# Pooling V on GpSimd instead of TensorE from group 7 on, with slack in a list schedule

## The chip, the core and the metric

One core of a Trainium2 chip runs the whole program. Times are device microseconds of one execution. Each figure is a median of several runs. A ratio is the mean time of one kernel's fast runs over the mean of the other kernel's fast runs of the same rounds, so it is not quite the ratio of the medians quoted beside it. The kernel before spreads by 0.9 to 2.2% in the four sets of its runs (352.6 to 360.3 us in the widest), so the ratios carry a 95% interval of about half a per cent to one per cent each way. In that widest set, which serves e1 to e4, three of seven runs (358.1 to 360.3 us) lie over 1.5% above the fastest, are classed slow and are left out, though their granted clock (0.98 to 0.99) is like that of the others; with them the ratios of e1 to e4 would be about 0.006 lower. Engines: PE is TensorE, ACT is ScalarE, DVE is VectorE, POOL is GpSimd, SP issues the DMAs (SPq in a trace is its queue).

## The reference, cut to what matters

```python
# 8 batches, 8 heads, 576 tokens, head size 64; factor 4
v_d = v.reshape(B, H, Sd, factor, D).mean(axis=3)     # the pooled V of this change; q_d, k_d likewise
out_d = sm_attn(q_d, k_d, v_d)                        # 144 pooled tokens
out_up = np.repeat(out_d, factor, axis=2)
scores = np.where(np.abs(pos[:, None] - pos[None, :]) < factor, scale * q @ k.T, -1e9)
x = out_up + softmax(scores) @ v                      # -> (4608 tokens, 512)
h = x @ w_in                                          # 512 x 2048
out = (h - np.tanh(h)) @ w_out                        # 2048 x 512
```

## The kernel before

The attention works on 32 pairs of heads, two pairs to a group, so 16 groups of four heads. The dense part works on nine blocks of 512 tokens and needs the attention's `xT` of the batches in its block. All work is entered into a small list scheduler. Each operation has an engine, an assumed duration, a priority and its dependencies. The scheduler plans start times and emits each engine's instructions in that order. On the chip each engine then works through its own stream in order and waits where it must (e1 below shows it).

```python
LAT = {"PE": 270, "ACT": 150, "DVE": 110, "POOL": 150, "SP": 50, "DMA": 1800}
...
            for u in users[i]:                       # in order(): when may a user start?
                same = self.ops[u][0] == eng and eng != "DMA"
                at[u] = max(at[u], end if same else end + self.LAT[eng])
...
    def pool_v(hb):                                  # V of a group pooled on PE
        def mm():
            for t in range(NT):                      # NT = 5
                T.matmul(pv[:, 0, :], pick[:, t, :], vw[w][:, :, t, 0:64], ...)
            T.matmul(pv[:, 1, :], pick[:, 5, :], vw[w][:, :, 4, 0:64], start=True, stop=True)
        op("PE", 750, mm, ..., writes=["ox"], pri=20 * hb - 1)       # takes PSUM bank ox
        op("ACT", 300, lambda: A.copy(out=vd[w][:, :, :, 0:64], in_=pv...), ...)
...
    def load_v4(n): ...          # V once more, as rows of four tokens, into qkn buffer 2
    def sum_v(n): ...            # two pairwise adds on POOL, the second writes vd
...
        if p % 2 == 0 and 1 < n < GV:
            pool_v(n)
...
        if nl[0] >= GV:
            load_v4(nl[0])
            sum_v(nl[0])
```

With `GV = 99` the last branch is never taken. After the output matmuls of a pair, DVE takes reciprocals and normalises into `ln`, which frees bank `ox`; SP issues a DMA transpose of `ln` into `lnT` (pairs 12 and up), and DVE adds the pooled part of `lnT`, each value repeated four times, to the rest of it, and writes `xT`. With `MERGE = 14`, the scores of pairs 14 and up go into both banks, `ts` and `ox`, in one block, so they wait for that same normalisation.

The softmax here doesn't subtract the row's maximum and nothing guards it: scores larger than these inputs give would overflow.

## Time and profile before

| | before |
|---|---|
| median of the three timed runs | 356.5 us (353.5 to 356.6) |
| span of the profiled run | 351.9 us |
| PE busy, and its idle time | 331.2 us, 20.7 us |
| PE idle from 140 to 260 us | 5.2 us |
| DVE / ACT / POOL busy | 212.5 / 210.8 / 110.9 us |

The prediction below reads this profile and shows the lines. One caution on reading them: this profile holds 1107 of the 1152 dense matmuls (556 + 551 rows), so a few of PE's short gaps are missing records and not idle time.

### The profile page before, as it was taken

What the parts mean: (1) busy time and instruction counts of PE and PEld (TensorE: products, weight loads), DVE (VectorE), ACT (ScalarE), POOL (GpSimd) and SP (SyncE); (2) the same over time, 40 slices, a digit from 0 to 9 for tenths busy, and PEclk for the clock granted to TensorE, in tenths of its full rate; (3) what the DMA queues carried; (4) which work ended last, traced back from release to release, by engine and by line L of the source; (5) the groups of instructions that cost most, each with busy time, mean ns of one, the idle gap of its engine ahead of it and who ended that gap; (6) DMA issues with size and microseconds to landing.
All of it is one profiled execution on the core that took longest, in us unless ns stands there. A gap on an engine that the chain in (4) does not pass through costs nothing.

```text
span 351.9 us, 6824 instructions
## 1 busy us (share of the span) xinstructions
PE 331.2 (94%) x2624; PEld 175.0 (50%) x2670; DVE 212.5 (60%) x360; ACT 210.8 (60%) x353; POOL 110.9 (32%) x140
## 2 busy tenths in 40 slices
PE   6978999989999999899989999999999999999995
PEld 2553555545555555455545555555444444444442
DVE  4774875748959676666767776956764343334300
ACT  2765988567966767565756767667634343444421
POOL 8434846664442152543434262622000000000000
PEclk9996999999999999999999999999999999999999
DMA  6999999999201759293939576525220100010012
GB/s 210 259 387 268 294 371 294 255 245 310 72 32 29 204 134 259 69 254 48 250 74 251 145 190 174 149 58 81 59 59 30 59 31 31 30 60 32 30 68 83
DMA packets 79278, 52.21 MB, mean 148 GB/s; under 512 B 62350, under 2 KB 62350, under 8 KB 79246
## 3 DMA queue, kind: packets, MB, share of 16 engines
q1 hardware_dynamic: 79246, 51.78, 54.3%
q8 instruction: 21, 0.34, 0.4%
q14 instruction: 11, 0.09, 0.1%
HBM read 37.74 MB, written 9.44 MB: 134 GB/s over the span
## 4 chain that ended last, share of the span: by engine, by line
PE 61%; DMA 15%; DVE 9%; SPq 8%; ACT 3%; issue 2%; POOL 1%; POOLq 0%; ACTq 0%; DVEq 0%
PE ps_hy L686 26%; PE ps_hy L658 26%; DMA lnT<-ln 4%; SPq L340 3%; SPq L364 3%; DMA vst<-in_v_dram 3%; DMA gT<-in_moe_w_out_dram 3%; DMA gT<-in_moe_w_in_dram 3%; DVE ln L592 2%; DVE gT L670 2%; PE ps_ts L452 2%; PE ps_ts L503 2%; PE ps_ox L575 2%; DMA qkn<-in_k_dram 2%; PE ps_ox L414 1%
## 5 line engine op out<-in xcount | busy, mean ns | idle before, releaser
L658 PE MATMUL ps_hy<-xT,w_in_sb 128*128 128x512 bf16 x556 | 143.8, 383 | 5.5 <-DVE xT L635 3.0
L686 PE MATMUL ps_hy<-w_out_sb,gT 128*128 128x512 bf16 x551 | 140.8, 379 | 1.6 <-issue 0.5
L670 DVE TENSOR_TENSOR gT<-ps_hy,uy 128x512 bf16<-128x512 f32 x144 | 96.7, 686 | 74.7 <-ACT uy L667 73.9
L667 ACT ACTIVATE uy<-ps_hy 128x512 f32<-128x512 f32 x144 | 84.1, 600 | 81.6 <-PE ps_hy L658 76.8
L658 PEld LDWEIGHTS <-w_in_sb 128*128 128x128 bf16 x576 | 54.0, 98 | 64.3 <-issue 6.7
L686 PEld LDWEIGHTS <-gT 128*128 128x128 bf16 x576 | 53.3, 98 | 58.4
L468 POOL TENSOR_TENSOR half<-qk 128x576 f32<-128x576 bf16 x29 | 35.2, 1215 | 78.4 <-ACT qk L458 72.1
L458 ACT COPY qk<-ps_ts 128x1152 bf16<-128x1152 bf16 x28 | 31.5, 1126 | 10.1 <-PE ps_ts L452 8.2
L542 ACT ACTIVATE E<-ps_ts 128x960 bf16<-128x960 f32 x30 | 29.0, 970 | 7.3 <-PE ps_ts L503 7.0
L592 DVE TENSOR_TENSOR ln<-ps_ox,r 128x896 bf16<-128x896 f32 x30 | 32.7, 1090 | 0.9
L697 ACT COPY uy<-ps_hy 128x512 f32<-128x512 f32 x36 | 21.1, 585 | 19.5 <-PE ps_hy L686 18.3
L399 POOL CAST vw<-vst 128x640 bf16<-128x640 f32 x31 | 23.5, 761 | 13.4 <-DMA vst<-in_v_dram 9.9
L546 DVE TENSOR_TENSOR E<-E,mask 128x960 bf16<-128x960 bf16 x28 | 21.3, 762 | 8.0 <-ACT E L542 7.7
L452 PEld LDWEIGHTS <-qr 128*128 128x128 bf16 x288 | 19.6, 103 | 11.0 <-DVE qr L436 5.6
L436 POOL CAST qr<-qkn 128x1152 bf16<-128x1152 f32 x14 | 16.0, 1144 | 24.9 <-DMA qkn<-in_k_dram 18.3
L611 DVE TENSOR_TENSOR xT<-lnT 128x480 bf16<-128x480 bf16 (+1 forms) x40 | 19.5, 495 | 6.7 <-DMA lnT<-ln 6.7
L436 DVE CAST qr<-qkn 128x1152 bf16<-128x1152 f32 x18 | 14.4, 801 | 13.6 <-DMA qkn<-in_q_dram 8.6
L473 POOL TENSOR_TENSOR qkd<-half 128x288 bf16<-128x288 f32 x30 | 21.7, 725 | 2.6 <-DVE half L468 1.3
L452 PE MATMUL ps_ts<-ident,qr 128*128 128x128 bf16 x252 | 19.6, 225 | 2.2 <-POOL vd L760 1.3
L575 PE MATMUL ps_ox<-vw,E 128*128 128x65 bf16 x300 | 18.8, 194 | 2.0 <-DVE E L564 1.9
L575 PEld LDWEIGHTS <-E 128*128 128x128 bf16 x300 | 15.6, 98 | 9.1 <-DVE E L564 2.5
L503 PEld LDWEIGHTS <-qk 64*128 64x128 bf16 x320 | 9.6, 96 | 15.7 <-issue 12.4
(83 smaller groups left out, 239.1 us busy)
## 6 DMA issues: line engine op xcount, KB each, us to landing
vst<-in_v_dram SPq DMA_DIRECT2D x62, 160.0 KB, 5.0
qkn<-in_q_dram SPq DMA_DIRECT2D x32, 288.0 KB, 3.4
qkn<-in_k_dram SPq DMA_DIRECT2D x32, 288.0 KB, 4.9
out_dram<-uy SPq DMA_DIRECT2D x36, 256.0 KB, 2.3
gT<-in_moe_w_in_dram SPq DMA_DIRECT2D x4, 1024.0 KB, 9.3
xT<-in_moe_w_out_dram SPq DMA_DIRECT2D x8, 256.0 KB, 4.4
gT<-in_moe_w_out_dram SPq DMA_DIRECT2D x2, 1024.0 KB, 9.6
lnT<-ln SPq DMA_TRANSPOSE x20, 3.0
```

Source lines behind the costliest of these rows:

```text
L399: P.choice([(eng, ns, lambda fn=fn: fn(out=vw[w][:, 2 * jj:2 * jj + 2, :, 0:64], in_=vst[s])) for eng, ns, fn in CAST_V[p >= NEARLY]], rea ...
L436: P.choice([(eng, ns, lambda fn=fn: fn(out=dst, in_=srt)) for eng, ns, fn in REORDER[n >= 2][i]], reads=[("qkn", sn, i, x) for x in range(2)],
L452: T.transpose(b16[:, 128 * a:128 * a + 128], qr[s][:, i, a, :], ident)
L458: fn(out=o.rearrange("p y (g a) -> p y g a", a=A6), in_=b16.rearrange("p (a g y) -> p y g a", a=A6, y=2))
L468: eng.tensor_tensor(out=half, in0=four[:, :, :, 0:2], in1=four[:, :, :, 2:4], op=ALU.add)
L542: op("ACT", 980, lambda: A.activation(out=e1, in_=ps[:, :, 0:480], func=AF.Exp, scale=SCALE), reads=ts, writes=[("E", se, 0)], pri=pri)
L575: T.matmul(po[:, hh, 65 * t:65 * t + 65], E[se][:, c:c + 128], vw[w][:, 2 * jj + hh, t, :], start=True, stop=True)
L592: op("DVE", 1090, lambda: V.tensor_tensor(out=ln[sl].rearrange("p n (h d) -> p h n d", d=D), in0=blocks[:, :, :, 0:64], in1=r[s].unsqueeze ...
L658: T.matmul(ps_hy[slot], w_in_sb[:, dc, fc * 128:(fc + 1) * 128], xT[dc][:, kb * 512:kb * 512 + 512], start=(dc == 0), stop=(dc == N_DC - 1))
L667: op("ACT", 490, lambda: A.activation(out=u[us], in_=ps_hy[slot], func=AF.Tanh), reads=[("hy", slot)], writes=[("u", us)], pri=-1)
L670: op("DVE", 620, lambda: V.tensor_tensor(out=gT[g][:, fc, :], in0=ps_hy[slot], in1=u[us], op=ALU.subtract), reads=[("hy", slot), ("u", us) ...
L686: T.matmul(ps_hy[slot], gT[g][:, fc, ts * 128:ts * 128 + 128], w_out_sb[:, fc, :], start=(fc == 0), stop=(fc == N_FF - 1))
```

## The change

Its intent is to take nine poolings off PE by summing V on the lightly used GpSimd, and to plan with more slack for results that come from a DMA or from GpSimd, so that no engine's stream puts a late result in front of ready work.

```diff
+        self.spare = (5000, {})
...
-                at[u] = max(at[u], end if same else end + self.LAT[eng])
+                lag = self.LAT[eng]
+                if self.spare[0] <= self.ops[u][4] < 5000:
+                    lag += self.spare[1].get(eng, 0)
+                at[u] = max(at[u], end if same else end + lag)
...
     P = Program()
+    P.spare = (140, {"DMA": 2500, "POOL": 1000})
...                                                  # assumed durations only:
-                 ..., (900, 250)[i], -30,           # load_v4
+                 ..., (1100, 350)[i], -30,
-            op("POOL", 1080, ...)                   # sum_v, first add; last add 580
+            op("POOL", 1330, ...)                   #                   last add 800
-    XOUT, T_OUT, AHEAD = 12, 1400, 5
-    MERGE, GV = 14, 99
-    XADD = [("DVE", (600, 170), V)]
+    XOUT, T_OUT, AHEAD = 12, 2000, 5
+    MERGE, GV = 14, 7
+    XADD = [("DVE", (800, 350), V)]
...
-              [("POOL", 720, GP.tensor_copy)]]      # second list of CAST_V
+              [("POOL", 790, GP.tensor_copy)]]
-              [("POOL", 1190, 750, GP)]]            # second list of ADDERS
+              [("POOL", 1190, 880, GP)]]
```

More of the change, by code (lines that the diff above doesn't have):

```diff
@@ L306, in load_v4 @@
             load(650, lambda to=to, rows=rows: nc.sync.dma_start(out=to, in_=rows),
-                 [("qkn", 2, i, y) for y in range(2)], (900, 250)[i], -30,
+                 [("qkn", 2, i, y) for y in range(2)], (1100, 350)[i], -30,
                  [("fl", 2 * n - AHEAD)])
@@ L316, in sum_v @@
             keys = [("qkn", 2, i, y) for y in range(2)]
-            op("POOL", 1080, lambda t=t: GP.tensor_tensor(
+            op("POOL", 1330, lambda t=t: GP.tensor_tensor(
                 out=t[:, :, 0:2], in0=t[:, :, 0:2], in1=t[:, :, 2:4], op=ALU.add),
@@ L324, in last @@
                                      in1=t[:, :, 1], op=ALU.add)
-            op("POOL", 580, last, reads=keys, writes=[("vd", w)], pri=pri)
+            op("POOL", 800, last, reads=keys, writes=[("vd", w)], pri=pri)
     def load_qk(n):
```

## The prediction

> **What bounds the kernel now.** I read the page first (busy shares, slices, chain of work that ended last), then the busy time by stretches, the list of PE's waits, and the timelines of PE, DVE, POOL and the SP queue around those waits. The page:
>
> ```profile
> span 351.9 us, 6824 instructions
> PE 331.2 (94%) x2624; PEld 175.0 (50%) x2670; DVE 212.5 (60%) x360; ACT 210.8 (60%) x353; POOL 110.9 (32%) x140
> ```
>
> PE is busy 94% of the span; no other engine passes 60%. Busy alone would prove little, since matmul ends are modelled, so the next view is where PE is not busy (columns: stretch, length, busy time by engine, granted clock, DMA share, GB/s):
>
> ```profile
> 0.00:40.00 40.00, 31.70 (x293) 17.92 (x297) 24.64 (x50) 24.83 (x42) 22.71 (x42) 0.91 0.96 282
> 40.00:80.00 40.00, 37.61 (x360) 21.32 (x365) 26.06 (x40) 29.83 (x53) 24.99 (x30) 1.00 1.01 292
> 80.00:140.00 60.00, 59.07 (x567) 33.19 (x574) 46.07 (x79) 43.73 (x75) 22.01 (x25) 1.00 0.54 145
> 140.00:260.00 120.00, 114.80 (x1014) 62.61 (x1030) 85.62 (x146) 78.59 (x128) 41.22 (x45) 1.00 0.58 135
> 260.00:340.00 80.00, 79.63 (x365) 36.28 (x371) 30.13 (x46) 32.09 (x56) 0.00 (x0) 1.00 0.12 42
> ```
>
> PE idles 8.3 us in the first 40 us and 2.4 us in the next 40, both with the DMA engines full (0.96 and 1.01): the load-bound start. It idles 0.9 us from 80 to 140, 5.2 us from 140 to 260, and 0.4 us in the last 80 us, which hold only the two dense products (L658, L686). That last stretch decides how the change counts: when the last attention pair ends, near 255 us, about 97 us of dense work is still queued. In the program attention has the better priority on PE and dense work fills the rest. So the time of attention's last step does not set the end. What sets it is the sum of PE's work and PE's idle time. Any PE microsecond removed in the middle brings the dense tail forward by one, and any new PE wait pushes it back by one. Engines beside PE count only through PE waits.
>
> **What the change touches.** GV goes from 99 to 7: for groups 7 to 15 (nine of them) V is no longer pooled on PE by the `pick` matmuls and copied by ACT; it is loaded a second time as rows of four tokens and summed by GpSimd. MERGE is 14 on both sides, so one score block a pair is already there from pair 14. The rest is schedule: operations with priority 140 to 4999 (attention from pair 14, preparation from about group 7) are planned 2.5 us later behind a DMA and 1.0 us later behind GpSimd, and several assumed durations are raised. The instructions stay the same there; only each engine's order moves.
>
> **Removed.** One pooling on PE and what follows it:
>
> ```profile
> 164.78 0.72 PE L414 MATMUL ps_ox<-vw,pick 128*128 128x256 bf16 x5
> 165.34 0.27 PE L416 MATMUL ps_ox<-vw,pick 128*128 128x256 bf16 x1
> 165.46 1.02 PE L658 MATMUL ps_hy<-xT,w_in_sb 128*128 128x512 bf16 x4
> ```
>
> From its first matmul to the next dense one is 0.68 us (not 0.72 + 0.27, because records overlap). The same distance at 115.45 and 197.37 is 0.67. There are ten such poolings from 102 us on, groups 6 to 15, and the change removes nine: 9 x 0.67 = 6.0 us of PE. It also removes nine ACT copies of 0.59 us (5.3 us, off the bound), and the turn of PSUM bank `ox` for the pooling. That turn has its own waits:
>
> ```profile
> PE ps_ox L414 <- DVE ln L592: 1.8, 2, 1.5
> PE ps_ox L575 <- DVE E L564: 1.7, 2, 1.1
> PE ps_ox L503 <- DVE ln L592: 0.4, 1, 0.4
> ```
>
> (PE's waits from 140 to 260 us: total, times, longest.) The first row, 1.8 us, is the pooling waiting for the bank to be read out by the previous pair. It goes with the pooling, although another PE instruction may meet part of the same lateness.
>
> **Added on GpSimd.** Per group two adds of 512 fp32 elements a partition and two of 256 (the second pair uses 32 partitions, which does not shorten it). The page's L468 row, a two-input add of 576 elements, takes 1215 ns, so 512 give 1.08 us; L473, 288 elements in 725 ns, gives 0.64 us for 256. Sum: 2 x (1.08 + 0.64) = 3.4 us a group; with the durations written in the diff (1.33 and 0.80), 4.3 us. The Trainium skill's "GPSIMD Engine Reference", section "Performance versus the Vector engine", gives 4497 ns for such an add of 2048 elements, so an estimate of 1.12 us for 512: the trace agrees. Groups are 16.0 us apart (115.45 to 243.82 in eight steps). GpSimd is busy 41.2 of 120 us from 140 to 260, or 5.5 us a group; it comes to 9 to 10 us, some 60%. It does not become the bound.
>
> **Added on DMA.** Per group 4 heads x 576 x 64 x 4 bytes = 590 KB, in 1 KB rows, nine times: 5.3 MB. At the 250 to 300 GB/s that the loaded slices show, that is 2.0 to 2.4 us a group, so the share of 0.58 goes to about 0.72. It fits on average; single landings come later.
>
> **What the skill says on waits.** "SBUF — State Buffer", section "Who interferes with whom", states that a DVE instruction with two SBUF inputs contends with a GpSimd instruction that reads SBUF, and that the later one blocks. The trace agrees strongly:
>
> ```profile
> 160.76 1.25 POOL L468 TENSOR_TENSOR half<-qk 128x576 f32<-128x576 bf16 x1 [1.29 <-ACT qk L458]
> 160.92 1.20 DVE L564 TENSOR_TENSOR E<-E,mask 128x192 bf16<-128x192 bf16 x1
> 162.18 0.20 PE L575 MATMUL ps_ox<-vw,E 128*128 128x65 bf16 x1 [0.55 <-DVE E L564]
> ```
>
> The mask multiply L564 has a median of 254 ns; here, beside a GpSimd add, it takes 1.20 us, and PE's output matmuls wait 0.55 us for it. The 1.1 us wait at 179.56 is the same collision. The second page that bears on it is "TensorE: Matmul & The Clock Gate", Part 2: matmuls stay in program order, so PE cannot step over such a wait to ready dense work; the bracket above, with 97 us of dense work queued, agrees. "DMA: Bandwidth & Descriptors", section "Specifications", names 512 B as the smallest transfer at full rate: the new rows are above it, the present V windows (256 B; 62350 of 79278 packets are under 512 B) are not. No run here shows yet what the new rows take.
>
> **The sum.** Pooling on PE: -6.0 us. Its own bank waits: -1.8, of which I count -1.3. Waits on late landings: the trace shows DVE waiting 6.4 us in all for the transposed `lnT` from 90 to 250 us, in nine waits, with mask and dense work behind it in DVE's queue. More planned slack (T_OUT from 1.4 to 2.0 and 2.5 on top) should spare PE a part of its remaining 3.4 us; I take -1.0. Against that, collisions: GpSimd's two-input adds take 3.9 us a group now and 7.3 to 8.2 afterwards, so about twice the chance that a mask multiply is held. PE lost 1.7 us to that in eight groups; doubled, +1.7, but nine fewer PE insertions and an earlier start of score blocks give back some, so +1.0. Net -7.3 us. I leave the first 80 us alone: the part of the plan before group 7 changes only by a few assumed durations, which I put at +-1 us either way.
>
> **Rivals.** (1) The collisions eat the gain: if the four new adds hold a mask multiply in every group at about 1 us a time, PE loses some 6 to 9 us and the time stays at 354 to 357. For: the 1.20 us instances and the in-order queues. Against: L564 is held in only 7 of the 23 cases I listed after 80 us, and only two of them made PE wait, because dense work stood between. (2) The new load takes the place of the pooling: `v4` lives in the third `qkn` buffer, so q and k keep only two, and each load of a group must wait for the sums of the group before; SP issues in order, so a blocked load also holds the `lnT` transposes behind it. DVE would then stall on `lnT`, and PE behind it. For: GpSimd already waits up to 7.9 us for k in this stretch. Against: DMA share is 0.58, and the gate on the transpose of pair 2n-5 already lets q and k start only about when the second-last buffer is free. It would leave 351 to 354. (3) The slack works better than I count: nearly all 5.2 us of idle goes and PE is solid from 80 us on; then 6.0 + 4.5 gives about 345.
>
> **Range and chances.** The three timed runs are 353.51, 356.51 and 356.61, and the profiled run 353.8; their mean is 355.1 and the median 356.5. From the median 356.5 - 7.3 = 349.2, from the mean 347.8. I predict 348.5. The range covers rival (3) below and most of rival (2) above: 345.0 to 352.5. The 2% line is 349.4 from the median and 348.0 from the mean, so the result sits on it; the sure part alone, 6.0 us, is 1.7%, and the bank waits bring it over. I give 0.52 to faster by over 2%, 0.45 to within 2%, 0.03 to slower.
>
> **What would show it.** The rows of L414, L416 and L421 should fall from 16 poolings to 7 (80 to 35 and 16 to 7 matmuls). New GpSimd rows on `vd<-qkn` and `qkn<-qkn` should read 18 each at 1.1 to 1.3 and 0.6 to 0.8 us, with GpSimd near 142 to 150 us busy. PE busy should be near 325 us, with PE's idle from 140 to 250 us at 3 to 4.5 us. The wait L414 <- L592 should be gone; L575 <- L564 should have grown. DVE's waits on `lnT` should be shorter. I am wrong if PE's idle there exceeds 8 us (then rival 1 or 2, told apart by what the wait names: L564 held by GpSimd, or a DMA), or if the stretch before 80 us moves by over 2 us.

## The result, and the profile after

The changed kernel takes 346.65 us (median of four runs, 346.3 to 347.1), against 356.2 us for the kernel before (353.5 to 356.6; a fourth run was made beside the change). The ratio is 0.9748, with a 95% interval of 0.9697 to 0.9799. Run again later it took 344.9 us, ratio 0.9718. The prediction was 348.5 us with a range of 345.0 to 352.5.

The head of the page:

```profile
span 344.5 us, 6832 instructions
PE 327.7 (95%) x2616; PEld 169.5 (49%) x2616; DVE 215.4 (63%) x360; ACT 204.5 (59%) x342; POOL 151.5 (44%) x179
```

GpSimd works 40.6 us more, ACT 6.3 us less, and PE is still the busiest engine. The same stretches as before (length, busy time by engine, granted clock, DMA share, GB/s):

```profile
0.00:40.00 40.00, 30.12 (x275) 17.07 (x276) 23.98 (x48) 22.67 (x38) 21.20 (x40) 0.87 0.91 278
40.00:80.00 40.00, 37.61 (x360) 20.69 (x358) 25.20 (x39) 28.76 (x50) 28.30 (x34) 1.00 0.99 294
80.00:140.00 60.00, 59.93 (x573) 32.88 (x574) 48.55 (x81) 43.56 (x74) 34.73 (x36) 1.00 0.64 171
140.00:260.00 120.00, 120.00 (x1017) 62.56 (x1016) 88.53 (x150) 77.95 (x127) 67.28 (x70) 1.00 0.67 168
```

From 140 to 260 us PE has no idle time at all, where it had 5.2 us (4.3 us of them named waits, the rest small gaps, some of them around missing records). The DMA share there rose from 0.58 to 0.67, and GpSimd from 41.2 to 67.3 us. The list of PE's waits between 80 and 260 us has one row left:

```profile
PE ps_ox L580 <- DVE E L569: 1.2, 1, 1.2
```

It begins at 78.9 us and so before the first of the new sums (86.0 us). In the stretch that the change is about, PE waits for nothing.

The new work on GpSimd (busy, mean ns of one, and its idle time before it):

```profile
L322 POOL TENSOR_TENSOR qkn<-qkn 128x512 f32<-128x512 f32 x9 | 12.3, 1364 | 1.8 <-DMA qkn<-in_v_dram 1.7
L322 POOL TENSOR_TENSOR qkn<-qkn 32x512 f32<-32x512 f32 x9 | 11.7, 1304 | 0.7
L328 POOL TENSOR_TENSOR vd<-qkn 32x256 bf16<-32x256 f32 x9 | 7.4, 827 | 0.7
L328 POOL TENSOR_TENSOR vd<-qkn 128x256 bf16<-128x256 f32 x9 | 7.3, 807 | 0.3
```

A group costs 1.36 + 1.30 + 0.83 + 0.81 = 4.3 us, and the adds on 32 partitions cost as much as those on 128. DVE's waits for `lnT` (6.7 us in ten waits from 80 to 270 us before) are gone altogether.

The first 40 us of this profile are worse than before (9.9 us idle against 8.3, clock 0.87 against 0.91). PE's program there is the same instruction for instruction: the two streams first differ after 28 dense matmuls. In this run one reorder of the start came later, PE waited 2.2 us for it instead of 0.9, and the granted clock was at half for 10.2 us instead of 6.8. The repeated run of the changed kernel (the last experiment) idled only 7.8 us in those 40 us. So this is mostly the chance of the start. The profiled run of the kernel before was also one of its quicker ones (353.8 us against a median of 356.2). For both reasons the span difference of 7.4 us understates the change.

### The profile page after: what moved, and what is told of

It is laid out like the page before. It is cut to its first block, busy times and chain, and to the rows that moved or that the text cites.

```text
span 344.5 us, 6832 instructions
## 1 busy us (share of the span) xinstructions
PE 327.7 (95%) x2616; PEld 169.5 (49%) x2616; DVE 215.4 (63%) x360; ACT 204.5 (59%) x342; POOL 151.5 (44%) x179
## 4 chain that ended last, share of the span: by engine, by line
PE 86%; DMA 6%; SPq 3%; POOL 1%; DVE 1%; ACT 1%; issue 1%; POOLq 0%; ACTq 0%; DVEq 0%
PE ps_hy L663 36%; PE ps_hy L691 36%; PE ps_ts L457 4%; DMA gT<-in_moe_w_in_dram 3%; PE ps_ts L508 3%; PE ps_ox L580 3%; SPq L369 2%; PE ps_ox L586 2%; DMA qkn<-in_k_dram 2%; DMA qkn<-in_q_dram 1%; SPq L345 1%; PE ps_ox L419 1%; PE ps_ox L527 1%; DVE xT L640 1%; PE ps_ox L635 0%
## 5 line engine op out<-in xcount | busy, mean ns | idle before, releaser
L663 PE MATMUL ps_hy<-xT,w_in_sb 128*128 128x512 bf16 x576 | 148.9, 385 | 4.8 <-DVE xT L640 4.0
L691 PE MATMUL ps_hy<-w_out_sb,gT 128*128 128x512 bf16 x576 | 145.6, 379 | 0.0
L473 POOL TENSOR_TENSOR half<-qk 128x576 f32<-128x576 bf16 x29 | 33.9, 1169 | 59.5 <-ACT qk L463 58.6
L404 POOL CAST vw<-vst 128x640 bf16<-128x640 f32 x31 | 24.5, 801 | 10.7 <-DMA vst<-in_v_dram 8.4
L322 POOL TENSOR_TENSOR qkn<-qkn 128x512 f32<-128x512 f32 (+1 forms) x18 | 24.0, 1334 | 2.5 <-DMA qkn<-in_v_dram 1.7
L616 DVE TENSOR_TENSOR xT<-lnT 128x480 bf16<-128x480 bf16 (+1 forms) x40 | 21.5, 549 | 0.0
L441 POOL CAST qr<-qkn 128x1152 bf16<-128x1152 f32 x14 | 17.1, 1219 | 8.8 <-PE ps_ts L457 5.0
L595 DVE RECIPROCAL r<-ps_ox 128x14 f32<-128x14 f32 x30 | 7.3, 243 | 20.5 <-PE ps_ox L586 18.6
```

The lines of the kernel that those rows point to most:

```text
L404: P.choice([(eng, ns, lambda fn=fn: fn(out=vw[w][:, 2 * jj:2 * jj + 2, :, 0:64], in_=vst[s])) for eng, ns, fn in CAST_V[p >= NEARLY]], rea ...
L441: P.choice([(eng, ns, lambda fn=fn: fn(out=dst, in_=srt)) for eng, ns, fn in REORDER[n >= 2][i]], reads=[("qkn", sn, i, x) for x in range(2)],
L473: eng.tensor_tensor(out=half, in0=four[:, :, :, 0:2], in1=four[:, :, :, 2:4], op=ALU.add)
L663: T.matmul(ps_hy[slot], w_in_sb[:, dc, fc * 128:(fc + 1) * 128], xT[dc][:, kb * 512:kb * 512 + 512], start=(dc == 0), stop=(dc == N_DC - 1))
L691: T.matmul(ps_hy[slot], gT[g][:, fc, ts * 128:ts * 128 + 128], w_out_sb[:, fc, :], start=(fc == 0), stop=(fc == N_FF - 1))
```

## The experiments

Three theories stood at the start. **Theory W**: the gain is PE work taken away, plus a few microseconds of waits that the slack removes, and the two add up. **Rival P**: the new plan gives the gain, and GpSimd's collisions eat what the pooling gives. **Rival B**: each part needs the other. Twelve runs were made, on three chips; e11 repeats e5, and e12 repeats the changed kernel. Ratios are to the kernel before, run beside them.

| | GV 99 | GV 7 |
|---|---|---|
| old plan | 1 | 1.0178 (e1) |
| new assumed durations only | not run | 0.9881 (e4) |
| slack only | 0.9843 (e2) | 0.9697 (e5, and again e11) |
| slack and new durations | 0.9942 (e3) | 0.9748, again 0.9718 (the change) |

### e1: the pooling moved, nothing else

```diff
-    MERGE, GV = 14, 99
+    MERGE, GV = 14, 7
```

> The kernel before with GV 99 to 7 and nothing else (no slack, old planned durations). Theory W (the gain is PE work: nine poolings of 0.67 us, waits as before): ratio to before 0.983, about -6 us, and PE's waits from 80 to 260 us stay near 4 us. Rival P (the gain comes from the new plan, GpSimd's collisions eat the pooling): ratio 0.995 to 1.005, with more waits of the output matmuls on the masked scores. Rival B (each needs the other): ratio above 1.0, waits on late landings.

Measured: 360.6 us (359.6 to 363.1), ratio 1.0178 (1.0084 to 1.0272). Six microseconds of PE work left the kernel, and it became slower. From 80 to 270 us, three rows of its list of waits (total, times, longest):

```profile
DVE xT L611 <- DMA lnT<-ln: 15.4, 6, 4.9
PE ps_ox L503 <- DVE ln L592: 10.6, 5, 4.2
PE ps_ox L522 <- POOL qkd L473: 2.9, 2, 1.4
```

The second follows from the first, as the longest of four like cases shows. SP's queue of this kernel:

```profile
151.98 3.67 SPq L364 DMA_DIRECT2D vst<-in_v_dram  x4
155.76 1.04 SPq L306 DMA_DIRECT2D qkn<-in_v_dram  x2
156.89 0.85 SPq L700 DMA_DIRECT2D out_dram<-uy  x2
157.83 13.35 SPq L600 DMA_TRANSPOSE lnT<-ln  x2
```

(The last row merges two transposes; the one that matters starts at 157.83.) Then DVE and PE of the same kernel:

```profile
166.11 2.13 DVE L611 TENSOR_TENSOR xT<-lnT 128x480 bf16<-128x480 bf16 x2 [4.94 <-DMA lnT<-ln]
168.16 0.23 DVE L590 RECIPROCAL r<-ps_ox 128x14 f32<-128x14 f32 x1
168.86 1.07 DVE L592 TENSOR_TENSOR ln<-ps_ox,r 128x896 bf16<-128x896 f32 x1
169.99 0.27 PE L503 MATMUL ps_ox<-qk 64*128 64x96 bf16 x2 [4.24 <-DVE ln L592]
```

Four V windows, the two new V loads and two stores are issued just ahead of the transpose. The DMA engines are full (share 1.14 from 155 to 160 us and 1.00 from 160 to 165), and `lnT` is usable 8.3 us after its issue began (166.11 - 157.83; the median of this run's transposes is 2.9 us). SP itself waited only 2.3 us in all for the buffer of the new loads from 80 to 270 us. DVE's stream has the add of `lnT` ahead of the reciprocal and the normalisation, though both concern a different pair and could have run: its output matmuls had ended at 162.83. PE's stream has the scores next, which need bank `ox`. So one late landing stops two engines that had other work.

Two things come on top. In two of the four cases PE then waited another 1.4 us for pooled keys (`qkd`, the third row): GpSimd had all four new sums ahead of them in its stream. And within 1.5 us of the end of each of the three longest stalls the granted clock fell to half for 3.4 us, where it stayed at full speed from 80 to 260 us in the kernel before, in e2 and in the changed kernel. The longest stall and what follows it (columns as before; the 0.67 is the mean of 3.4 us at half and the rest at full clock):

```profile
165.00:170.00 5.00, 0.76 (x12) 0.28 (x11) 3.89 (x6) 1.16 (x2) 3.63 (x4) 0.99 0.00 0
170.00:175.00 5.00, 5.00 (x28) 2.26 (x28) 2.32 (x4) 1.98 (x5) 0.00 (x0) 0.67 0.72 183
```

After the fourth, of 1.9 us, it did not fall. So each long stall of this run was paid twice. An estimate from these profiles, with the first 80 us left aside: PE's idle time from 80 to 270 us rose from 6.2 (some of it missing records) to 14.2 us (+8.0), three times 3.4 us at half clock cost 5.1 us of work, and 6.0 us of pooling went: about 7 us slower, where the ratio says some 6.

At the same phase of the kernel before, the transpose stands behind the V windows and one store, without the two new loads:

```profile
151.49 4.05 SPq L364 DMA_DIRECT2D vst<-in_v_dram  x4
155.64 0.47 SPq L700 DMA_DIRECT2D out_dram<-uy  x1
156.21 9.24 SPq L600 DMA_TRANSPOSE lnT<-ln  x2
```

There DVE began the add at 160.34, 4.1 us after the issue, having waited 0.25 us. Two pages of the Trainium skill fit this. "DMA: Bandwidth & Descriptors", section "Queues, rings and completion order", states that SP owns one ring on each DMA engine and that an engine consumes a ring's descriptors in ring order; the 8.3 us against a median of 2.9 us agrees, though no run separated the order in the ring from the mere amount of data. "TensorE: Matmul & The Clock Gate", in the table of specifications at its head, lists VectorE's queue as strict FIFO; the 4.94 us wait, with a reciprocal behind it whose input was ready for the last 3.3 us, agrees. Theory W failed here, and so did rival P: its ratio of 0.995 to 1.005 lies outside the interval, and PE's wait on the masked scores was 0.3 us. Rival B's "waits on late landings" is what happened.

### e2: the slack, nothing else

```diff
+    P.spare = (140, {"DMA": 2500, "POOL": 1000})     # and its use in order(); GV and durations as before
```

> The kernel before with only the slack in the list schedule (2.5 us behind a DMA, 1.0 us behind GpSimd, from priority 140 on); GV stays 99, planned durations stay old. Theory W with slack removing PE's late waits: 3 to 4 us of the 5 us idle from 140 to 260 us go, ratio 0.990. Rival P: the main gain is here, ratio 0.980. Rival B: ratio 1.00.

Measured: 348.9 us (348.0 to 350.8), ratio 0.9843 (0.9756 to 0.9930). No instruction is added or taken away. The stretch from 140 to 260 us:

```profile
140.00:260.00 120.00, 119.82 (x1050) 64.52 (x1049) 87.09 (x152) 79.88 (x130) 41.09 (x43) 1.00 0.56 136
```

PE's idle time fell from 5.2 to 0.2 us, and DVE has no wait for `lnT` left from 80 to 270 us. The ratio lies between those of theory W (0.990) and rival P (0.980), and its interval holds both; rival B's 1.00 lies outside.

### e3 and e4: the new assumed durations, without GV and without the slack

```diff
-    MERGE, GV = 14, 7                                     # e3: on the changed kernel
+    MERGE, GV = 14, 99
-    P.spare = (140, {"DMA": 2500, "POOL": 1000})          # e4: on the changed kernel
```

Of e3:

> The changed kernel with GV set back to 99: slack and new planned durations, pooling on PE throughout. Theory W: the changed kernel's time plus about 6 us, ratio to before 0.990. Rival P: as fast as the changed kernel, ratio 0.975. Rival B: ratio 1.00.

Of e4:

> The changed kernel with the slack line taken out: GV 7 and the new planned durations. Theory W with slack worth 3 to 4 us: ratio 0.983 to 0.985, with PE waits from 80 to 260 us back at 3 to 5 us. Rival P: ratio 0.995. If the new durations do the work of the slack: ratio 0.975, same as the changed kernel.

Measured, e3: 352.7 us (352.4 to 353.1), ratio 0.9942 (0.9854 to 1.0029). That is 3.9 us more than e2 on the same chip, and the two kernels differ only in assumed durations. Theory W's 0.990 and rival B's 1.00 both lie in the interval, rival P's 0.975 does not. Measured, e4: 350.5 us (median of its three fast runs, 350.0 to 350.9), ratio 0.9881 (0.9792 to 0.9970); its profiled run took 384.0 us at a granted clock of 0.84, so its profile is not compared. The interval does not separate theory W from rival P, and 0.975 lies outside it. e4 is 10.2 us faster than e1 on the same chip: with GV 7 and no slack, the new durations (among them a transpose planned at 2.0 instead of 1.4 us and longer adds behind it) do much of what the slack does. Which of them does it was not separated.

At this point I suspected that the new durations harm the first 80 us: in the profiles of the changed kernel and of e3, the 17th tanh of the dense part (the 16th, counted from zero, in an expectation below) ended at 78.6 and 76.4 us, against 74.1, 74.8 and 72.7 us in the kernel before, e1 and e2. That is 1.6 to 5.9 us later; the "4.5 us" of the next expectation is the changed kernel against the kernel before. The next call tested this as theory D.

### e5: GV and slack, all durations as before

> GV 7 plus the slack, with all planned durations as in the kernel before. So far: slack alone took 8 us off and left PE almost no wait from 80 to 260 us; GV alone cost 3 us because DVE waited up to 4.9 us for a late lnT; and both kernels with the new planned durations (the changed one, and it with GV 99) reached the same point of the dense work 4.5 us later by 80 us than those without. Theory D (the new durations harm the plan of the first 80 us, the rest adds up): slack alone minus 6 us, about 343 us, ratio to before 0.965. Rival N (the added loads and sums eat what the pooling gave, whatever the durations): as slack alone, 348 to 349 us, ratio 0.984. Rival L (the new late durations are needed beside GV): 350 us or more, PE waiting on ln and lnT.

Measured: 344.5 us (343.4 to 344.8), ratio 0.9697 (0.9641 to 0.9754). That is 4.4 us under e2 by the medians (another chip), where the pooling was put at 6 us; rival N's 0.984 and rival L's time lie outside the interval. Once the slack is there, most of the pooling's worth does add up.

### e6: slack, and the pooling dropped with nothing in its place

```diff
-        if p % 2 == 0 and 1 < n < GV:                 # on e2
+        if p % 2 == 0 and 1 < n < 7:
```

> Slack alone, and the pooling of groups 7 to 15 dropped without a replacement (a wrong result on purpose: old pooled values are used). The value of the removed PE work by itself: nine times 0.67 us, so 6 us under slack alone, 342.5 us, ratio 0.966. If the list schedule lands unluckily or PE meets other waits in place of the pooling: 2 to 3 us under slack alone.

Measured: 342.2 us (341.2 to 343.1), ratio 0.9629 (0.9562 to 0.9696). Its output is wrong, which doesn't matter for the time. Against e2, which ran on another chip, the medians differ by 6.7 us and the ratios by 2.1 points (some 7.6 us), or 5.4 us with the slow runs of e2's set kept, so the nine poolings are worth some 5 to 8 us where no new wait replaces them. The predicted 6.0 us lies in that.

### e7: the changed kernel with two GpSimd durations set back

```diff
-              [("POOL", 790, GP.tensor_copy)]]
+              [("POOL", 720, GP.tensor_copy)]]
-              [("POOL", 1190, 880, GP)]]
+              [("POOL", 1190, 750, GP)]]
```

> The changed kernel with two planned GpSimd durations set back (the V cast 790 to 720 and the second q/k add 880 to 750), the only ones among the new that can move the plan of the first 80 us. Theory D: the dense work is 4 us further at 80 us and the time is 342.5 to 343.5, ratio 0.964. Rival (the loss of the first 80 us is chance of the loads, or the late durations matter more): 346 to 347, ratio 0.975.

Measured: 349.2 us (347.6 to 350.3), ratio 0.9833 (0.9769 to 0.9896). Theory D's number missed by 6 us, and its rival's 346 to 347 us by 2. The 17th tanh did come earlier (75.6 us), and the kernel still was 4.7 us slower than e5 on the same chip. PE's named waits from 80 to 270 us are 3.3 us in total against 0.8 us in e5; the rest of the 4.7 us no wait of the profiles names. Why this plan is worse stays open.

### e8: slack, with the second load and the sums on top while PE goes on pooling

```diff
-    MERGE, GV = 14, 99                                # on e2
+    MERGE, GV = 14, 7
-        if p % 2 == 0 and 1 < n < GV:
+        if p % 2 == 0 and n > 1:
```

> Slack alone, with the second load of V and the GpSimd sums added from group 7 on while PE goes on pooling too (the pooled values of PE come last and are used). The price of the added work by itself. Theory D: it hides beside PE, 348 to 350 us, ratio 0.984 to 0.987. Rival N: 353 us or more, with PE waits on masked scores held by GpSimd, or on ln behind a late lnT.

Measured: 350.1 us (349.2 to 352.1), ratio 0.9868 (0.9805 to 0.9931). Against e2 (another chip) the added work costs 1.2 us by the medians. The other measure of it, e5 against e6 on one chip, gives 2.3 us (344.45 - 342.15). So under the slack the load and the sums cost 1 to 2 us; this is what theory D expected, and rival N's 353 us or more did not come. In none of these profiles does a wait of that size name them, and the two profiled spans of e5 and e6 are 0.3 us apart, so I cannot say where it lies.

### e9 and e10: the two halves of the slack

```diff
-    P.spare = (140, {"DMA": 2500, "POOL": 1000})      # on e5
+    P.spare = (140, {"DMA": 2500})                    # e9
+    P.spare = (140, {"POOL": 1000})                   # e10
```

Of e9:

> GV 7 and only the half of the slack that stands behind a DMA (2.5 us), old planned durations. GV alone lost time where DVE waited up to 4.9 us for lnT and PE then 4.2 us for ln. Theory L (late landings are what the slack is for): 344 to 345 us as with both halves, ratio 0.970, DVE hardly waiting for lnT. Rival C (collisions of GpSimd adds with DVE multiplies, which only the GpSimd half plans for): 352 us or more, ratio 0.99 or above.

Of e10:

> GV 7 and only the half of the slack that stands behind GpSimd (1.0 us), old planned durations. Theory L: little better than GV alone, 356 to 361 us, ratio 1.005 to 1.018, with DVE waiting 10 us or more for lnT and PE for ln. Rival C: 344 to 347 us, ratio 0.970 to 0.978.

Measured: e9 347.0 us (345.1 to 348.6), ratio 0.9772 (0.9721 to 0.9822); e10 358.8 us (357.2 to 362.4), ratio 1.0121 (1.0066 to 1.0176). The waits of DVE for `lnT` from 80 to 270 us, first in e9:

```profile
DVE xT L616 <- DMA lnT<-ln: 2.2, 2, 1.6
```

and in e10:

```profile
DVE xT L616 <- DMA lnT<-ln: 12.7, 6, 3.2
```

Theory L holds for most of the times: with the half behind a DMA the kernel takes 347.0 us, where GV alone took 360.6, and the half behind GpSimd alone leaves it slower than before. Beside the first half, the second gives another 3 us (e11 below, same chip), more than theory L expected. The profiles lean to collisions there: PE waits 1.4 us for the small mask multiply in e9 against 0.2 us in e11, and DVE is busy 7.1 us longer with the same instructions (223.4 against 216.3 us). No run tested it.

In e10 theory L's path is only half right. DVE did wait over 10 us for `lnT`, but PE waited just 0.2 us for `ln`. Its largest wait was for GpSimd's pooled keys:

```profile
PE ps_ox L527 <- POOL qkd L478: 4.0, 3, 2.4
```

Next came 3.8 us for the subtraction after the tanh. GpSimd waited 33.4 us for loads of k, against 13.1 us in the kernel before, and half-clock stretches of 3.4 us came three times, as in e1. So `lnT` is not the only way by which e10 loses time; how much goes by each was not separated.

### e11 and e12: e5 and the changed kernel side by side

Of e11:

> The kernel with GV 7 and the whole slack, old planned durations, run again beside the changed kernel on one chip. If the new planned durations really cost time: 344 to 345 us and 2 us under the changed kernel. If that was a difference of chips: equal within 0.5 us.

Of e12, the changed kernel unedited:

> The changed kernel itself, unedited, run again beside the others. 346 to 347 us, ratio 0.975; a profile of its first 80 us that again has the 16th tanh near 78 us if the slower start belongs to its plan, near 75 if it was chance.

Measured: e11 344.0 us (343.2 to 345.0), ratio 0.9697; e12 344.9 us (343.6 to 346.2), ratio 0.9718. The ranges overlap and the means differ by 0.8 us, so the old durations are not shown to be better beside GV and slack; neither expectation of e11 (2 us, or within 0.5) was met exactly, and e12 came out 1 to 2 us under its own. In e12's profile the 17th tanh ended at 75.9 us. Theory D falls: the late start of the first profile of the changed kernel was mostly chance. No version here clearly beats the changed kernel.

## Why the prediction was right, and where its steps were not

The time was right: 346.65 us inside 345.0 to 352.5, and the ratio 0.9748 on the faster side of the 2% line, to which I had given 0.52. Its sum was -7.3 us; the ratio stands for about 9 us. The wait of the pooling for its bank was gone, and DVE's waits for `lnT` with it, as written. By its steps:

- **What sets the end.** Right. PE is the bound; with the waits gone, PE is busy for the whole stretch from 140 to 260 us (327.7 us in all, where I wrote near 325). The attention's last normalisation ended 9.5 us later than before (267.8 against 258.3 us) and the kernel still ended 7.4 us earlier.
- **Removed poolings, -6.0 us.** Right in size, some 5 to 8 us (e6 against e2). But I called it "the sure part alone, 6.0 us, is 1.7%", and that step is wrong: by itself, moving the pooling made the kernel 1.8% slower (e1).
- **Rival 2.** I argued against it with an average, a DMA share of 0.58. In e1 its stalls came true, by way of full DMA engines in front of `lnT` rather than by a blocked buffer (2.3 us of SP's waits): ten microseconds of full engines, `lnT` 8.3 us after its issue, DVE and then PE stopped in order, and the clock at half after it. I named the wait but not this path, nor the clock. The 7.9 us wait for k that I cited lies before 140 us; from 140 to 260 us the longest was 1.4 us. An average share does not rule out a full stretch in front of one small transfer.
- **Bank waits and late landings, -1.3 and -1.0 us.** Mis-sized. I expected 3 to 4.5 us of PE's idle time to stay; the slack alone took it from 5.2 to 0.2 us, and 1.6% of the time (5.6 us of some 356). My third rival ("nearly all 5.2 us of idle goes and PE is solid") described it.
- **Collisions, +1.0 us.** Not confirmed. In the kernel after, the small mask multiply's median duration rose from 254 to 339 ns, so more of them are held. PE's wait on it from 140 to 260 us went from 1.7 us to none, where I expected it to grow. The whole added work costs 1 to 2 us under the slack (e8, e5 against e6), with no wait that names collisions; that its size comes near my +1.0 us is luck.
- **GpSimd and DMA.** GpSimd is busy 151.5 us, just above the 142 to 150 us I gave; a group's sums take 4.3 us, the figure from the diff's own durations, not my 3.4 us. Scaling from another add of the trace and from the skill's figure gave 1.08 and 1.12 us for 512 elements, and 1.30 to 1.36 us were measured. The DMA share is 0.67, not 0.72. The poolings fell to 7 and the new rows are 18 each, as written.
- **The first 80 us, +-1 us.** My own sign of being wrong, a move of over 2 us, showed in the first profile: the 17th tanh came 4.5 us late. In the repeat it was 1.8 us (75.9 against 74.1 us), so most of it was chance, and what is left is not explained.

So the number came out partly by luck, through errors of opposite sign: a gain counted as sure that needs the slack, and a slack counted too low.

## What to carry to other kernels

Where engines work in order and one of them is the bound, what an operation costs depends on what stands behind it in each stream: taking six microseconds of work off the bound made this kernel slower until the plan expected late landings, and then the same edit paid most of its worth. A stall of the bound engine can cost more than its length, as the half clock after e1's stalls shows. Try a removal and the slack for the work that replaces it as a factorial, not one after the other. And judge a transfer by what is queued in front of it in its ring, not by the mean share of the DMA engines; replans of a list schedule alone moved this kernel by 3 to 5 us, so repeat before explaining such a difference.

## What the Trainium skill lacked or had wrong

- "GPSIMD Engine Reference", section "Performance versus the Vector engine": it gives a figure for 2048 elements and none for fewer partitions. A two-input add on 32 partitions takes about as long as on 128; the runs show 1304 ns against 1364 ns for 512 fp32 elements, and 827 against 807 ns for 256. The estimate from its figure, 1.12 us for 512 elements, was too low: the fastest of 18 adds took 1.26 us, and the mean on 128 partitions, 1364 ns, is 1.21 times the estimate, measured beside other work.
- "DMA: Bandwidth & Descriptors": the page gives no landing time for a DMA transpose. Here a 128 x 896 bf16 transpose landed in a median of 2.9 to 3.0 us, and in up to 8.3 us with six loads and two stores just ahead of it on SP's queue (e1).
